# A new step list with paired banks, loads of the first pair on three queues, last tiles through ACT alone

## The chip, the cores and the metric

The kernel runs on one core of one Trainium2 chip. The time is the device time of one execution in microseconds; the median of the runs is compared. The engines are PE (TensorE: matmuls, with its weight loads as PEld), DVE (VectorE), ACT (ScalarE), POOL (GpSimd) and SP (SyncE, which only issues transfers here). DMA queues of SP, ACT and POOL move data between HBM and SBUF; matmul results lie in PSUM.

## The reference

q, k and v are 8 batches x 8 heads x 1152 positions x 64. Neighbouring queries are averaged, so 576 queries meet 1152 keys. The output of attention, 4608 tokens x 512, goes through a multiplicative FFN without a nonlinearity.

```python
q_pool = q.reshape(B, H, S // 2, 2, D).mean(axis=3)
scores = scale * np.matmul(q_pool, k.transpose(0, 1, 3, 2))
attn = softmax(scores)                     # with 1e-9 in the sum
x = np.matmul(attn, v)                     # to [4608, 512]
a = x @ w1; b = x @ w2
out = (a * b @ w3) @ w_out
```

All inputs and outputs are float32; the kernel computes in float16 with float32 sums.

## The kernel before

Two heads make a pair, so there are 32 pairs (four to a batch). The scores of all pairs are one long row of blocks, cut into 324 **slots** of 512 columns for both heads: PE multiplies keys by queries into a two-bank PSUM tile `psc` (L284) and ACT writes the exponential to a ring in SBUF (L289). An **`a` unit** (128 of them, four to a pair) multiplies 128 queries' exponentials by v with a column of ones beside it (L346), and DVE divides (L351, L358); the result is turned into `xT`, by PE for the first eight pairs and by a DMA transpose issued on SP after that (L303). The last 64 queries of two pairs form a **`c` unit** (L373).

The FFN is a list of 196 **steps**: eight "turn" and eight "mult" that form w3 times w_out, then for each of nine chunks of 512 tokens eight times "a" (w1) and "b" (w2), four matmuls of 512 columns each, and four "o" of eight matmuls. An "a" result is copied to `asb`, a "b" result is multiplied by it into `gT`, an "o" result is scaled into `osb` and stored. DVE does these, except in the **tail** (after the last slot), where ACT copies "a", and DVE and ACT each scale half of an "o". The very last step (`fill_last`) runs in two halves of 256 columns.

PSUM has eight banks: three two-bank buffers `psc` (`double()`) and two one-bank buffers `one` (`single()`).

The order on PE is written out by hand in a string, `PLAN`, one letter a step:
- `s`: a slot; `a`: an `a` unit; `c`: a `c` unit; `k`, `j`: turning keys and queries of a pair on PE (`transp_pe`, `transp_rest`); `t`: turning a finished result now.
- `f`: one FFN step in a `one` bank. `F`: one FFN step in a `psc` buffer of which one bank is used. `D`: two FFN steps, one in each half of the same `psc` buffer. `d`: two FFN steps in two `one` banks (not in either plan).

Other engines follow PE's order: their instructions stand in the order in which the string's steps are recorded. The tile framework sets the waits between engines.

For pair 0, loads are split so that a first slot can start early: keys 0 to 2 of nine blocks (`KA = 3`), the two heads' queries `qst0`, and a short rest `qtl0`. ACT casts the first keys (L552), DVE adds neighbouring queries (L555, L556), and PE turns both into one `psc` tile (L246), which is copied out as `kqT` in two pieces (L249).

Of the kernel before, what the change touches and what calls it, by code (L numbers as in the profile page):

```python
# [13 lines left out]

GRP = 2
PLAN = (
    "ksssjsssssksssssfaFasssfsssaksffssasacsssasakassfssfssfassakassfsssffsssffsssafkascsssasaFasssfs"
    "sakassfkssafsssafcsssfFtasssafssaFasssafssafssafssafsssfasscfasssafasssffssfsssafsssafsssafsssaf"
    "fsssafcsssafssafasssaffsssaaFasssffssffssscfasssaffsssafassfsssafsssafsssafassscfasssaaFfsssaffs"
    "ssaffsssaffsssaffssscfasssaaFasssaffsssffsssafsssafsssaasfssscfasssaffsssaffsssaffsssaffsssaffss"  # L20
    "saaFcsssaaFasssaffsssfFasssafsssafasssffssscfasssaffsssaffsssaffsssffFfsssaffsssaaFassscfasssafa"
    "sssafsssfassaassfsssaffsssfaFassscffsssffssffsssafssafasssafassaDaassscfasssafsssfssfasssaffsssa"
    "ffsssaffsssaffsssaaFcsssafFfsssfaDasssaffsssfssaFcFaFaFaFaFFFFFFFFFFFFFFFFFFFFFFFFFFFFFFFFFFFFFF"
)


# [91 lines left out]
def kernel(  # L118
# [11 lines left out]
    nc = tc.nc  # L130
# [14 lines left out]
    QM = 4  # L145
# [98 lines left out]
    def turn_blocks(pt, kq16, blocks):  # L244
        for c in blocks:
            nc.tensor.transpose(pt[:, c * 128:c * 128 + 128], kq16[:, c].rearrange("p u d -> p (u d)"), ident16)  # L246

    def copy_blocks(eng, kqT, pt, c0, c1):
        eng(out=kqT[:, c0:c1].rearrange("p c i -> p (c i)"), in_=pt[:, c0 * 128:c1 * 128])  # L249
# [3 lines left out]
    def transp_pe(p):  # L253
        kq16 = pairs[p]
        kqT = att.tile([128, NB, 128], FP16, tag="kqT", bufs=3)
        pt = double().rearrange("p b c -> p (b c)").bitcast(FP16)
        if p == 0:
            turn_blocks(pt, kq16, list(range(KA)) + list(range(NJ, NB)))
            copy_blocks(nc.vector.tensor_copy, kqT, pt, NJ, NB)
            copy_blocks(nc.scalar.copy, kqT, pt, 0, KA)  # L260
            rest[0] = (kq16, kqT)
        else:
            turn_blocks(pt, kq16, range(NB - 1, -1, -1))
            for c0, c1 in ((8, NB), (0, 4), (4, 8)):
                copy_blocks(nc.vector.tensor_copy, kqT, pt, c0, c1)
        pairs[p] = kq_views(kqT)
# [131 lines left out]
    def pieces(c):  # L398
        a = (c * CH) % XR
        if a + CH <= XR:  # L400
            return [(0, a, CH)]
        return [(0, a, XR - a), (XR - a, 0, CH - (XR - a))]
# [39 lines left out]
                    nc.tensor.matmul(pt[:, d0:d0 + n], wt[:, mc, ft * 128:ft * 128 + 128], xT[:, mc, a:a + n],  # L442
                                     start=(mc == 0 and d0 == 0), stop=(mc == NC - 1), skip_group_check=True)

    def mm_rows(two, pts):
        kind, c, ft = two[0]
        for half in range(2):
            for m in range(NC if kind == "a" else NF):
                for d0, a, n in (pieces(c) if kind == "a" else [(0, 0, dm)]):
                    for u in range(2):  # L450
                        hs = slice(u * 64, u * 64 + 64)
                        x = (half + u) % 2
                        if kind == "a":
                            wt = (w1sb, w2sb)[x]
                            lhsT, rhs = wt[hs, m, ft * 128:ft * 128 + 128], xT[hs, m, a:a + n]
                        else:
                            t0 = two[x][2] * 128
                            lhsT, rhs = gTs[c][hs, m, t0:t0 + 128], T16[hs, m, :]
                        nc.tensor.matmul(pts[x][:, d0:d0 + n], lhsT, rhs, start=(half == 0 and m == 0 and d0 == 0),
                                         stop=(half == 1 and m == (NC if kind == "a" else NF) - 1), skip_group_check=True)  # L460

    def put(step, pt):
        kind, c, ft = step
        tail = st["s"] == NS
        if kind == "turn":
            w3T[ft] = msb.tile([128, NF, 128], FP16, tag="w3T", bufs=2, name="w3T")
            nc.vector.tensor_copy(out=w3T[ft].rearrange("p a i -> p (a i)"), in_=pt.bitcast(FP16))
        elif kind == "mult":
            nc.vector.tensor_copy(out=T16[:, ft, :], in_=pt)
        elif kind == "a":  # L470
            asbs[ft] = msb.tile([128, CH], FP32, tag="asb", bufs=2, name="asb")
            (nc.scalar.copy if tail else nc.vector.tensor_copy)(out=asbs[ft], in_=pt)  # L472
        elif kind == "b":
            nc.vector.tensor_tensor(out=gTs[c][:, ft, :], in0=pt, in1=asbs.pop(ft), op=ALU.mult)  # L474
        else:
            osb = msb.tile([128, dm], FP32, tag="osb", bufs=3, name="osb")
            if tail:
                nc.vector.tensor_scalar_mul(out=osb[:, 0:256], in0=pt[:, 0:256], scalar1=1.0 / (SCL * SCL))
                nc.scalar.mul(out=osb[:, 256:512], in_=pt[:, 256:512], mul=1.0 / (SCL * SCL))
                store(nc.sync, c * CH + ft * 128, osb)  # L480
            else:
                nc.vector.tensor_scalar_mul(out=osb, in0=pt, scalar1=1.0 / (SCL * SCL))  # L482
                store(nc.gpsimd, c * CH + ft * 128, osb)

    def take():
        step = steps[st["f"]]
        st["f"] += 1
        ready(step)
        return step

    def fill_one(bank):
        st["mode"] = 1
        step = take()
        mm(step, bank)
        put(step, bank)

    def fill_last():
        _, c, n = take()
        osb = msb.tile([128, dm], FP32, tag="osb", bufs=3, name="osb")
        for x in range(2):  # L500
            cs = slice(x * 256, x * 256 + 256)
            pt = double()[:, 0, 0:256]
            for f_ in range(NF):
                nc.tensor.matmul(pt, gTs[c][:, f_, n * 128:n * 128 + 128], T16[:, f_, cs],  # L504
                                 start=(f_ == 0), stop=(f_ == NF - 1))
            if x == 0:
                nc.scalar.mul(out=osb[:, cs], in_=pt, mul=1.0 / (SCL * SCL))
            else:
                nc.vector.tensor_scalar_mul(out=osb[:, cs], in0=pt, scalar1=1.0 / (SCL * SCL))
        store(nc.sync, c * CH + n * 128, osb)  # L510

    def fill_two(banks):
        kinds = [s_[0] for s_ in steps[st["f"]:st["f"] + 2]]
        if st["mode"] == 0 and kinds in (["a", "b"], ["o", "o"]):
            two = [take(), take()]
            pts = banks()
            mm_rows(two, pts)
            for step, pt in zip(two, pts):
                put(step, pt)
        else:  # L520
            pts = banks()
            for pt in pts:
                fill_one(pt)


    def w3_load(r):
# [6 lines left out]
    kst0 = att.tile([128, 2, NJ, D], FP32, tag="kst")  # L533
    qst0 = att.tile([128, 2, QM * 2 * D], FP32, tag="qst")
    qtl0 = att.tile([QT, 2, 2 * D], FP32, tag="qtl")
    for u in range(2):
        nc.sync.dma_start(out=qst0[:, u], in_=q[0, u, 0:QM * 256].rearrange("(p c) d -> p (c d)", p=128))
    nc.scalar.dma_start(out=kst0[:, :, 0:KA], in_=k_view(0)[:, :, 0:KA])
    nc.scalar.dma_start(out=qtl0, in_=q[0, 0:2, QM * 256:S].rearrange("u (p t) d -> p u (t d)", t=2))
    nc.sync.dma_start(out=kst0[:, :, KA:NJ], in_=k_view(0)[:, :, KA:NJ])  # L540
    load_kq(1, nc.sync, nc.sync)
# [85 lines left out]
    for op in PLAN:  # L627
        if op == "s":
            slot()
        elif op == "a":  # L630
            av_unit(st["a"])
            st["a"] += 1
            st["mode"] = 1
        elif op == "c":
            av_tails(st["c"])
            st["c"] += 1
            st["mode"] = 2
        elif op == "f":
            fill_one(single())
        elif op == "F":  # L640
            if st["f"] == len(steps) - 1:
                fill_last()
            else:
                fill_one(double()[:, 0, :])
        elif op == "D":
            def banks():
                two = double()
                return two[:, 0, :], two[:, 1, :]
            fill_two(banks)
        elif op == "d":  # L650
            fill_two(lambda: (single(), single()))
        elif op == "k":
            transp_pe(st["k"])
            st["k"] += 1
            st["mode"] = 1
        elif op == "j":
            transp_rest()
            prepare(2)
            st["mode"] = 1
        elif op == "t":  # L660
            one = single()
            turn_mm(one)
            turn_copy(one)
            st["mode"] = 1
        if not flag and st["a"] == NU and st["c"] == (NP // GRP if GRP else 0) and not turns:
            count_bad()
        if "okh" in flag and "badi" not in flag and st["f"] >= len(steps) - 20:
            read_bad()
# [35 lines left out]
```

## Time and profile before

| what | us |
|---|---|
| runs (3): median | 418.66 |
| lowest, highest | 417.94, 419.73 |
| profiled execution | 419.7 |
| its span in the profile | 417.5 |
| PE busy | 399.7 |
| ACT busy | 323.0 |
| DVE busy | 208.8 |

The span runs from the first to the last instruction of the program; 2.2 us of the profiled execution lie around it. Busy times overlap between engines. A line of a timeline gives start, duration, engine, source line, operation, output and inputs, and in brackets how long the engine sat idle before and who released it. A line of the waits gives the waiting instruction, the releaser, the total in us, the count and the longest. L numbers are lines of the kernel before.

### The profile page before, as it was taken

What the parts mean: (1) busy time and instruction counts of PE and PEld (TensorE: products, weight loads), DVE (VectorE), ACT (ScalarE), POOL (GpSimd) and SP (SyncE); (2) the same over time, 40 slices, a digit from 0 to 9 for tenths busy, and PEclk for the clock granted to TensorE, in tenths of its full rate; (3) what the DMA queues carried; (4) which work ended last, traced back from release to release, by engine and by line L of the source; (5) the groups of instructions that cost most, each with busy time, mean ns of one, the idle gap of its engine ahead of it and who ended that gap; (6) DMA issues with size and microseconds to landing.
All of it is one profiled execution on the core that took longest, in us unless ns stands there. A gap on an engine that the chain in (4) does not pass through costs nothing.

```text
span 417.5 us, 12618 instructions
## 1 busy us (share of the span) xinstructions
PE 399.7 (96%) x5273; PEld 231.6 (55%) x5273; DVE 208.8 (50%) x565; ACT 323.0 (77%) x354; POOL 166.8 (40%) x211
## 2 busy tenths in 40 slices
PE   2899999999999999999999999999999999999993
PEld 1466666656556556564556555556776555554442
DVE  1156566666355635654456445644654465453331
ACT  3979897999998998888998889789896886622321
POOL 3979877733173318331635064117430600000000
PEclk9999999999999999999999999999999999999998
DMA  8999998999897999977999689949994910320302
GB/s 258 258 304 275 264 297 298 340 242 308 222 201 207 235 242 304 249 212 200 256 272 280 160 226 290 295 91 292 233 254 98 202 52 15 64 65 0 100 2 108
DMA packets 90895, 86.34 MB, mean 207 GB/s; under 512 B 59664, under 2 KB 64272, under 8 KB 90832
## 3 DMA queue, kind: packets, MB, share of 16 engines
q1 hardware_dynamic: 81616, 59.85, 59.9%
q0 software_dynamic: 8800, 25.37, 21.2%
q8 instruction: 43, 0.70, 0.7%
q10 hardware_dynamic: 416, 0.26, 0.2%
q14 instruction: 20, 0.16, 0.2%
HBM read 67.11 MB, written 9.44 MB: 183 GB/s over the span
## 4 chain that ended last, share of the span: by engine, by line
PE 93%; ACT 3%; DMA 1%; DVE 1%; issue 0%; SPq 0%; DVEq 0%; ACTq 0%
PE one L442 20%; PE psc L284 20%; PE one L346 19%; PE one L436 10%; PE psc L442 10%; PE psc L436 5%; PE one L433 3%; ACT ring L289 3%; PE one L373 3%; PE psc L246 2%; DMA qst<-in_q_dram 1%; PE one L430 1%; PE one L314 0%; PE psc L504 0%; PE psc L433 0%
## 5 line engine op out<-in xcount | busy, mean ns | idle before, releaser
L289 ACT ACTIVATE ring<-psc 128x1024 f16<-128x1024 f32 x324 | 307.1, 1028 | 46.6 <-PE psc L284 46.3
L284 PE MATMUL psc<-kqT 64*128 64x512 f16 (+7 forms) x1152 | 95.6, 291 | 2.8 <-ACT kqT L249 1.1
L346 PEld LDWEIGHTS <-ring 128*128 128x128 f16 x2304 | 79.7, 98 | 26.6 <-issue 17.1
L346 PE MATMUL one<-vaug,ring 128*128 128x65 f16 x2304 | 91.2, 194 | 0.0
L284 PEld LDWEIGHTS <-kqT 64*128 64x128 f16 x1152 | 43.4, 95 | 48.9 <-issue 30.3
L226 POOL CAST kq<-kst 128x1152 f16<-128x1152 f32 x31 | 35.7, 1150 | 58.2 <-DMA kqT<-kq 48.7
L413 POOL DMA_DIRECT2D out_dram<-osb x22 | 12.1, 551 | 110.7 <-DVE osb L482 82.2
L442 PE MATMUL one<-xT,w1sb 128*128 128x512 f16 (+1 forms) x220 | 49.5, 352 | 0.0
L442 PE MATMUL one<-xT,w2sb 128*128 128x512 f16 (+1 forms) x216 | 49.4, 356 | 0.0
L351 DVE RECIPROCAL rzall<-one 128x2 f32<-128x2 f32 x128 | 21.5, 168 | 54.5 <-PE one L346 38.5
L436 PE MATMUL one<-T,gT 128*128 128x512 f16 x192 | 45.4, 379 | 0.0
L442 PEld LDWEIGHTS <-w1sb 128*128 128x128 f16 x320 | 28.3, 97 | 27.2 <-DVE xb L358 3.5
L442 PEld LDWEIGHTS <-w2sb 128*128 128x128 f16 x320 | 28.0, 97 | 25.3 <-issue 2.3
L436 PEld LDWEIGHTS <-gT 128*128 128x128 f16 x280 | 25.5, 98 | 28.9 <-issue 1.5
L472 DVE COPY asb<-one 128x512 f32<-128x512 f32 x48 | 33.2, 691 | 16.5 <-PE one L442 16.5
L474 DVE TENSOR_TENSOR gT<-one,asb 128x512 f16<-128x512 f32 x48 | 33.2, 691 | 16.5 <-PE one L442 16.5
L219 POOL TENSOR_TENSOR kq<-qst 128x512 f16<-128x512 f32 x31 | 39.4, 1271 | 1.6 <-DMA qst<-in_q_dram 1.5
L234 POOL CAST vaug<-vst 128x1152 f16<-128x1152 f32 x32 | 36.6, 1143 | 5.6 <-DMA vst<-in_v_dram 5.5
L482 DVE TENSOR_SCALAR osb<-one 128x512 f32<-128x512 f32 x24 | 16.6, 691 | 34.7 <-PE one L436 34.7
L358 DVE TENSOR_TENSOR xb<-one,rzall 128x128 f16<-128x128 f32 x96 | 28.0, 291 | 3.3
L474 DVE TENSOR_TENSOR gT<-psc,asb 128x512 f16<-128x512 f32 x24 | 16.6, 691 | 18.5 <-PE psc L442 18.5
L442 PE MATMUL psc<-xT,w2sb 128*128 128x512 f16 (+1 forms) x104 | 24.6, 362 | 0.8 <-DVE asb L472 0.8
(71 smaller groups left out, 266.4 us busy)
## 6 DMA issues: line engine op xcount, KB each, us to landing
vst<-in_v_dram SPq DMA_DIRECT2D x25, 576.0 KB, 5.2
kst<-in_k_dram SPq DMA_DIRECT2D x23, 576.0 KB, 6.0
qst<-in_q_dram SPq DMA_DIRECT2D x23, 512.0 KB, 7.6
out_dram<-osb POOLq DMA_DIRECT2D x22, 256.0 KB, 5.7
kst<-in_k_dram POOLq DMA_DIRECT2D x8, 576.0 KB, 9.0
qst<-in_q_dram POOLq DMA_DIRECT2D x8, 512.0 KB, 9.7
vst<-in_v_dram POOLq DMA_DIRECT2D x7, 576.0 KB, 8.0
out_dram<-osb SPq DMA_DIRECT2D x10, 256.0 KB, 2.1
```

What stands on the lines that cost most here:

```text
L219: eng.tensor_tensor(out=kq16[:, NJ:NJ + QM].rearrange("p c u d -> p u c d"), in0=qv[:, :, :, 0], in1=qv[:, :, :, 1], op=ALU.add)
L226: nc.gpsimd.tensor_copy(out=kq16[:, 0:NJ].rearrange("p c u d -> p u c d"), in_=kst)
L234: nc.gpsimd.tensor_copy(out=va[:, :, :, 0:D], in_=vs.pop(p).rearrange("p u (c d) -> p u c d", d=D))
L284: nc.tensor.matmul(psc[:, u, f - s * G:f - s * G + ln], kT2[u * 64:u * 64 + 64, jt, :], qpT[u * 64:u * 64 + 64, i0:i0 + ln], start=True, s ...
L289: nc.scalar.activation(out=ring[:, :, r0:r0 + G], in_=psc, func=AF.Exp, bias=0.0, scale=SCALE)
L346: nc.tensor.matmul(one[:, u * E1:u * E1 + E1], ring[:, u, c0:c0 + 128], va[:, u, jt, :], start=(jt == 0 and u == 0), stop=(jt == NJ - 1), ...
L351: nc.vector.reciprocal(out=rz, in_=av[:, :, D:E1].rearrange("p u o -> p (u o)"))
L358: nc.vector.tensor_tensor(out=xbt, in0=av[:, :, 0:D], in1=rz.unsqueeze(2).to_broadcast([128, 2, D]), op=ALU.mult)
L436: nc.tensor.matmul(pt, gTs[c][:, f_, ft * 128:ft * 128 + 128], T16[:, f_, :], start=(f_ == 0), stop=(f_ == NF - 1))
L442: nc.tensor.matmul(pt[:, d0:d0 + n], wt[:, mc, ft * 128:ft * 128 + 128], xT[:, mc, a:a + n], start=(mc == 0 and d0 == 0), stop=(mc == NC - ...
L472: (nc.scalar.copy if tail else nc.vector.tensor_copy)(out=asbs[ft], in_=pt)
L474: nc.vector.tensor_tensor(out=gTs[c][:, ft, :], in0=pt, in1=asbs.pop(ft), op=ALU.mult)
```

## The change

Four parts.

1. A new `PLAN`. Counts of letters, before and after: `s` 324 and 324, `a` 128 and 128, `c` 16 and 16, `k` 8 and 8, `f` 134 and 128, `F` 58 and 40, `D` 2 and 14, `t` 1 and 2. Behind the last `s` before: `aFcFaFaFaFa` and 38 times `F`. After: `ffcFaDDfaFaffDFFFaFffFDFDFDFFFDfDFFfDDFF`.
2. The special matmul order for two steps at once (`mm_rows`) and the letter `d` are removed; `D` now always runs its two steps one after the other with `fill_one`.
3. Pair 0: the first keys are loaded through POOL's queue, the two heads' queries through SP's and ACT's, one each. PE turns the keys first and ACT copies them, then PE turns the queries and DVE copies them.
4. The end: both halves of the last tile are scaled by ACT, and the stores of the last two tiles are issued by ACT instead of SP.

```diff
@@ PLAN: last two of seven lines
-    "sssafsssfassaassfsssaffsssfaFassscffsssffssffsssafssafasssafassaDaassscfasssafsssfssfasssaffsssa"
-    "ffsssaffsssaffsssaaFcsssafFfsssfaDasssaffsssfssaFcFaFaFaFaFFFFFFFFFFFFFFFFFFFFFFFFFFFFFFFFFFFFFF"
+    "saffsssfasssafsssfasssafssscfasssafFasssaffsssafssaaFfsssaffsssfFfssscfasssafFasssafsssafsssfass"
+    "safsssafcsssaaDfsssaffsssafDfsssaaDasssfDasssffcFaDDfaFaffDFFFaFffFDFDFDFFFDfDFFfDDFF"
...
@@ transp_pe, p == 0
-            turn_blocks(pt, kq16, list(range(KA)) + list(range(NJ, NB)))
-            copy_blocks(nc.vector.tensor_copy, kqT, pt, NJ, NB)
-            copy_blocks(nc.scalar.copy, kqT, pt, 0, KA)
+            turn_blocks(pt, kq16, range(KA))
+            copy_blocks(nc.scalar.copy, kqT, pt, 0, KA)
+            turn_blocks(pt, kq16, range(NJ, NB))
+            copy_blocks(nc.vector.tensor_copy, kqT, pt, NJ, NB)
...
@@ put, "o" in the tail
-                store(nc.sync, c * CH + ft * 128, osb)
+                store(nc.scalar if st["f"] >= len(steps) - 1 else nc.sync, c * CH + ft * 128, osb)
...
@@ fill_last
-            if x == 0:
-                nc.scalar.mul(out=osb[:, cs], in_=pt, mul=1.0 / (SCL * SCL))
-            else:
-                nc.vector.tensor_scalar_mul(out=osb[:, cs], in0=pt, scalar1=1.0 / (SCL * SCL))
-        store(nc.sync, c * CH + n * 128, osb)
+            nc.scalar.mul(out=osb[:, cs], in_=pt, mul=1.0 / (SCL * SCL))
+        store(nc.scalar, c * CH + n * 128, osb)
@@ fill_two
-        kinds = [s_[0] for s_ in steps[st["f"]:st["f"] + 2]]
-        if st["mode"] == 0 and kinds in (["a", "b"], ["o", "o"]):
-            two = [take(), take()]
-            pts = banks()
-            mm_rows(two, pts)
-            for step, pt in zip(two, pts):
-                put(step, pt)
-        else:
-            pts = banks()
-            for pt in pts:
-                fill_one(pt)
+        for pt in banks:
+            fill_one(pt)
@@ first loads
-    for u in range(2):
-        nc.sync.dma_start(out=qst0[:, u], in_=q[0, u, 0:QM * 256].rearrange("(p c) d -> p (c d)", p=128))
-    nc.scalar.dma_start(out=kst0[:, :, 0:KA], in_=k_view(0)[:, :, 0:KA])
+    nc.gpsimd.dma_start(out=kst0[:, :, 0:KA], in_=k_view(0)[:, :, 0:KA])
+    for u, eng in enumerate((nc.sync, nc.scalar)):
+        eng.dma_start(out=qst0[:, u], in_=q[0, u, 0:QM * 256].rearrange("(p c) d -> p (c d)", p=128))
     nc.scalar.dma_start(out=qtl0, in_=q[0, 0:2, QM * 256:S].rearrange("u (p t) d -> p u (t d)", t=2))
     nc.sync.dma_start(out=kst0[:, :, KA:NJ], in_=k_view(0)[:, :, KA:NJ])
@@ D
-            def banks():
-                two = double()
-                return two[:, 0, :], two[:, 1, :]
-            fill_two(banks)
-        elif op == "d":
-            fill_two(lambda: (single(), single()))
+            two = double()
+            fill_two((two[:, 0, :], two[:, 1, :]))
```

More of the change, by code (lines that the diff above doesn't have):

```diff
@@ L16 @@
 PLAN = (
[L17 to L21, printed above, removed]
-    "sssafsssfassaassfsssaffsssfaFassscffsssffssffsssafssafasssafassaDaassscfasssafsssfssfasssaffsssa"
-    "ffsssaffsssaffsssaaFcsssafFfsssfaDasssaffsssfssaFcFaFaFaFaFFFFFFFFFFFFFFFFFFFFFFFFFFFFFFFFFFFFFF"
+    "ksssjsssssksssssfaFasssfstssaksafsssfasscsassaksafsssffsssfassaksafsssfssaFacsssfasssfakkassfsss"
+    "afsssftFkssafsssfFasssafcsssafssfassafssfasssafssaFasssfFasssfassaFcsssafsssfasssfasssafsssafssf"
+    "FasssafcsssffssfassafssfasssafassfasssafcsssfFasssafassfasssafsssafsssfasssafsssafcsssafssafasss"
+    "faFasssffssffsssaffsssaaFcsssfFfsssaaFasssfssfsssfasssfasssaffssscfasssaffsssafassaassffsssaffss"
+    "safcsssaaFasssaffsssaffsssafsssfasssfasssafsssffcsssfFfsssfFasssaaFasssaffsssaaFcsssfFasssaaFass"
+    "saffsssfasssafsssfasssafssscfasssafFasssaffsssafssaaFfsssaffsssfFfssscfasssafFasssafsssafsssfass"
+    "safsssafcsssaaDfsssaffsssafDfsssaaDasssfDasssffcFaDDfaFaffDFFFaFffFDFDFDFFFDfDFFfDDFF"
 )
@@ L443, in mm @@
                                      start=(mc == 0 and d0 == 0), stop=(mc == NC - 1), skip_group_check=True)
[L445 to L449, printed above, removed]
-                    for u in range(2):
[L451 to L455, printed above, removed]
-                        else:
[L457 to L460, printed above, removed]
     def put(step, pt):
@@ L505, in fill_last @@
                                  start=(f_ == 0), stop=(f_ == NF - 1))
-            if x == 0:
-                nc.scalar.mul(out=osb[:, cs], in_=pt, mul=1.0 / (SCL * SCL))
-            else:
-                nc.vector.tensor_scalar_mul(out=osb[:, cs], in0=pt, scalar1=1.0 / (SCL * SCL))
-        store(nc.sync, c * CH + n * 128, osb)
-    def fill_two(banks):
-        kinds = [s_[0] for s_ in steps[st["f"]:st["f"] + 2]]
-        if st["mode"] == 0 and kinds in (["a", "b"], ["o", "o"]):
-            two = [take(), take()]
-            pts = banks()
-            mm_rows(two, pts)
-            for step, pt in zip(two, pts):
-                put(step, pt)
-        else:
-            pts = banks()
-            for pt in pts:
-                fill_one(pt)
+            nc.scalar.mul(out=osb[:, cs], in_=pt, mul=1.0 / (SCL * SCL))
+        store(nc.scalar, c * CH + n * 128, osb)
+    def fill_two(banks):
+        for pt in banks:
+            fill_one(pt)
     def w3_load(r):
@@ L535 @@
     qtl0 = att.tile([QT, 2, 2 * D], FP32, tag="qtl")
-    for u in range(2):
-        nc.sync.dma_start(out=qst0[:, u], in_=q[0, u, 0:QM * 256].rearrange("(p c) d -> p (c d)", p=128))
-    nc.scalar.dma_start(out=kst0[:, :, 0:KA], in_=k_view(0)[:, :, 0:KA])
+    nc.gpsimd.dma_start(out=kst0[:, :, 0:KA], in_=k_view(0)[:, :, 0:KA])
+    for u, eng in enumerate((nc.sync, nc.scalar)):
+        eng.dma_start(out=qst0[:, u], in_=q[0, u, 0:QM * 256].rearrange("(p c) d -> p (c d)", p=128))
     nc.scalar.dma_start(out=qtl0, in_=q[0, 0:2, QM * 256:S].rearrange("u (p t) d -> p u (t d)", t=2))
```

## Prediction

> **What bounds the kernel now.** I read the page first: shares, slices, chain.
>
> ```profile
> span 417.5 us, 12618 instructions
> PE 399.7 (96%) x5273; PEld 231.6 (55%) x5273; DVE 208.8 (50%) x565; ACT 323.0 (77%) x354; POOL 166.8 (40%) x211
> PE   2899999999999999999999999999999999999993
> ACT  3979897999998998888998889789896886622321
> PE 93%; ACT 3%; DMA 1%; DVE 1%; issue 0%; SPq 0%; DVEq 0%; ACTq 0%
> ```
>
> PE is busy in every slice but the first two and the last, and the chain that ended last is PE for 93%. So what counts is how long PE takes through its own list, where it waits, how early it starts and what follows its last matmul. A busy PE need not be at its peak, so next I put the PE's matmuls beside the plan, letter by letter, and measured each step from its first matmul to the next step's. After 24 us the same pair of neighbours takes the same time nearly everywhere: a four-matmul step 0.86, an eight-matmul step 1.73, an `a` 0.56; a slot's two to four matmuls 0.23. Entering a run of slots costs 0.09 and leaving it 0.09. Both plans hold the same 5273 matmuls.
>
> Then the waits of PE from 24 to 365 us, and from 365 us on. The first answer has two rows, the second none:
>
> ```profile
> PE psc L442 <- DVE gT L474: 0.8, 1, 0.8
> PE psc L442 <- DVE asb L472: 0.8, 1, 0.8
> ```
>
> These are the only two places where PE stands still after the start, and they are exactly the two `D` in the plan of before. The timeline around the second:
>
> ```profile
> 350.45 1.02 PE L442 MATMUL psc<-xT,w1sb 128*128 128x512 f16 x4
> ...
> 351.51 0.69 DVE L472 COPY asb<-psc 128x512 f32<-128x512 f32 x1 [0.32 <-PE psc L442]
> 352.25 1.02 PE L442 MATMUL psc<-xT,w2sb 128*128 128x512 f16 x4 [0.78 <-DVE asb L472]
> ```
>
> A `D` takes one two-bank `psc` buffer and runs two FFN steps into its halves. The second step does not follow at 350.45 + 0.86 = 351.31. It starts when the copy out of the first half is over, at 352.25: **0.94 us lost**. The other `D` took 1.82 (311.57 to 313.39) against 0.88 for its neighbours: 0.94 again. Single steps (`f`, `F`) take a fresh buffer each; the 38 `F` that close the plan of before, from 370.56 us on, ran without a gap.
>
> **The `D` steps.** The new plan has 14 in place of 2; 10 of them stand after the last slot, where nothing but FFN steps is left. In the built list of the changed kernel, the first matmul of every one of the 14 second halves carries a wait on DVE or ACT, the engine that reads the first half. Nothing can cover it: PE goes through its list in order, and behind the waiting matmul stands all the rest of PE's work. What the first half is decides the price:
> - 4 before the last slot, copy or product by DVE as in the row: 4 x 0.94 = 3.76.
> - 4 in the tail begin with an "a" step, which ACT copies in 0.58 instead of 0.69: 0.94 - 0.11 = 0.83, x4 = 3.32.
> - 3 begin with a "b". DVE's product took 0.69, but began 0.12 after the matmuls' end (373.15 + 1.03 to 374.29) instead of 0.04: about 1.01, x3 = 3.03.
> - 3 begin with an "o", read by DVE and then by ACT, one after the other:
>
> ```profile
> 384.58 0.42 DVE L478 TENSOR_SCALAR osb<-psc 128x256 f32<-128x256 f32 x1 [0.97 <-PE psc L436]
> 385.03 0.38 ACT L479 ACTIVATE osb<-psc 128x256 f32<-128x256 f32 x1 [2.46 <-DVE osb L478]
> 371.62 0.58 ACT L472 COPY asb<-psc 128x512 f32<-128x512 f32 x1 [2.24 <-PE psc L442]
> ```
>
> From 384.58 to 385.41 is 0.83 in place of 0.69: 1.08, x3 = 3.24. (The last row is the 0.58 used above.)
>
> Sum 13.35; less the two of before (1.88): **+11.5 us**. No row of before shows two `D` in succession, which the new plan has twice; both ends there are "no more than the sum" and, were a third buffer late, one more 0.9.
>
> **The rest of the list.** Runs of slots fall from 119 to 118: -0.2. A tail unit `c` followed by one single-bank step and an `a` makes the `a` wait 0.1 for the `c`'s bank (0.96 instead of 0.86); this pattern falls from 8 to 3: -0.5. An extra early `t` moves two small matmuls. The removed two-bank row-split matmuls were not reached by the plan of before. Hidden waits of the new order are bounded from below by 0, since before had none to remove, and from above by rows for what could come late: the transposed kq lands 6.7 us after its issue (median), and in the new list at least 8.5 us of PE work lie between issue and use (9.2 before); the first FFN step of a chunk stands 13 us or more behind the last `a` that feeds it through a DMA transpose (10.9 before; median landing 4.5, worst 9.5). I take 0, and keep 3 us for the range. ACT has 20% of its time free and hides the reordered exponentials.
>
> **The start.** The rows up to the first slot:
>
> ```profile
> 5.28 0.51 ACT L552 CAST kq<-kst 128x384 f16<-128x384 f32 x1 [1.98 <-DMA kst<-in_k_dram]
> 6.60 0.71 PE L246 MATMUL psc<-ident,kq 128*128 128x128 f16 x5 [0.25 <-DVE kq L555]
> 7.35 0.49 DVE L249 COPY kqT<-psc 128x640 f16<-128x640 f16 x1 [0.58 <-PE psc L246]
> 7.87 0.48 ACT L249 COPY kqT<-psc 128x384 f16<-128x384 f16 x1 [2.08 <-DVE kqT L249]
> 8.41 1.46 PE L284 MATMUL psc<-kqT 64*128 64x512 f16 x10 [1.09 <-ACT kqT L249]
> ```
>
> Before, the late second half of q sets the first slot: added at 6.54, turned, copied twice in a row. With keys first, ACT's copy comes ahead of the query turns, and as built these turns wait for it (one `psc` tile again). The new chain is: keys land, cast 0.51, three turns 0.50, ACT copy 0.48, five turns 0.71, DVE copy 0.49, and five hand-overs of about 0.05: 2.94 from the landing of the keys to the first slot. The keys' first part now goes through POOL's queue. No row shows that transfer there; the nearest ones:
>
> ```profile
> kst<-in_k_dram ACTq DMA_DIRECT2D x1, 192.0 KB, 4.5
> w3c<-in_moe_w_dram POOLq DMA_DIRECT2D x4, 512.0 KB, 7.5
> ```
>
> Lower bound: 4.5 as on ACT's queue, landing at 5.25, first slot at 8.2, 0.2 earlier than before. Upper bound: the fastest 512 KB load on POOL's queue, 6.4, landing at 7.15, first slot at 10.1, +1.7. I take the middle, 5.5: **+0.8**. All of it reaches the end, since from there ACT's and PE's work follow one upon the other. The transfer's issue (0.7 to 0.9 on POOL) pushes the identity and memsets to about 3 us, ahead of their use at 5.85; were that cover gone it would cost those 0.8. Q halves on two queues land together rather than one after the other; they are no longer last.
>
> **The end.** Last matmul, then copy, issue, landing. The last half goes to ACT (0.38) instead of DVE (0.42 at 410.75), and ACT issues its store itself, saving a hand-over of 0.06: -0.1. The store before it is now issued by ACT too, 0.3 to 0.5 between ACT's pieces of the last two tiles; the first of these ended 0.5 before the last matmul, so this room is just enough: 0, at worst +0.1. I take 0 for the two together.
>
> **Sum.** +11.5 - 0.2 - 0.5 + 0.8 = +11.6. The profiled execution took 419.7 (span 417.5 and 2.2 around it), so it would become 431.3. The median of before, 418.66, lies 1.0 under that execution: predicted **430.2 us**.
>
> **Rivals.**
> 1. *The two halves of a `D` do not block each other.* They lie in different banks; if the wait were met when PE comes to it, both the 12 new and the two old stalls vanish: 418.66 - 1.9 - 0.7 + 0.8 = 416.9, with the start's lower bound 415.9. This is the other side, and it decides where the reader's end comes before PE's 0.22 per matmul runs out. Against it: the two rows of waits and the built waits. Chance 0.05, 0.02 of it faster by over 0.5%. The Trainium skill, "PSUM — Partial Sum Buffer", section "PSUM bank collisions raise a hardware error", asks for ordering by bank and quadrant only and calls different banks clean; by that no wait is needed, and the time would be this rival's. The trace has the program order whole tiles all the same: 0.78 us of waiting for a reader of the other bank.
> 2. *The PE clock falls in the tail.* PE turned 128-wide blocks every 0.107 us up to 22.9 us, with gaps of 0.3 to 1 us in its work, and every 0.056 after; it reached that pace only after 3.2 us without a gap. If ten gaps of about 1 us put it back for some 3 us each, at half pace, 1.5 us apiece: +15, 445. Against: the pace stayed at 0.216 per 512 columns after both gaps of before. Chance 0.04. The Trainium skill, "TensorE: Matmul & The Clock Gate", section "A second HAM failure mode: psum-queue depth-cycling", tells of such falls from frequent short idling between groups of matmuls. The single gaps of before neither show nor exclude it.
> 3. *The new order has waits of its own* (a late transpose, an exponential not ready): 3 to 6 us more, 433 to 436. Chance 0.06.
> 4. *Half the stalls are absorbed*, say since DVE and ACT are idle enough in the tail to read sooner: +6, 424. But the durations used are already those of idle engines. Chance 0.04.
>
> **How the numbers follow.** The forecast, 427 to 433, holds 0.81. Range 426.5 to 433.5: the unknown of the start (-1.0, +0.9), hidden waits (+3) and the spread of the runs (about 1), less a fifth of the shares on each `D`. Half a percent, 2.1 us, is about what can be told from no change. Slower: forecast, 2, 3 and 4, 0.95; faster 0.02; same 0.03.
>
> **What would show it.** PE's waits after 24 us should list 14 rows' worth of second halves, about 0.8 to 1.1 each, ten behind the last slot; the first slot between 8.2 and 10.1; steps elsewhere at 0.86 and 1.73. It is wrong if the second halves of `D` start 0.86 or 1.73 after the first, if matmuls in the tail come slower than 0.216, or if PE waits elsewhere.

## The result, and the profile after

The changed kernel took 430.06 us (median of 4 runs, 427.5 to 430.61), the kernel before 418.58 (4 runs) beside it: ratio 1.0259, 95% interval 1.0212 to 1.0306. It is 11.5 us slower. The profiled execution took 429.98 with a span of 427.8, so span against span it is 10.3 more.

From the page of the changed kernel, the span, PE's busy slices and the shares of the chain that ended last:

```profile
span 427.8 us, 12633 instructions
PE   1899999999999999999999999999999988898885
PE 92%; ACT 3%; DVE 2%; DMA 1%; issue 1%; DVEq 0%; POOLq 0%
```

Where PE before had a 9 in every slice between the start and the last, now seven of the last eight show an 8 or a 5: most of the loss lies in the last fifth. The chain shows DVE at 2% instead of 1%: PE stands behind it. PE's waits from 24 us on say for whom (waiting instruction, releaser, total us, times, longest):

```profile
PE psc L443 <- DVE gT L458: 4.0, 5, 0.9
PE psc L437 <- ACT osb L463: 2.8, 3, 0.9
PE psc L443 <- ACT asb L456: 2.7, 4, 0.7
PE psc L437 <- DVE gT L458: 0.9, 1, 0.9
PE psc L443 <- DVE asb L456: 0.8, 1, 0.8
```

5 + 3 + 4 + 1 + 1 are 14 waits, one for each `D`, and there is no other row. (The rows count idle time from the modelled end of the last matmul; the loss against an undisturbed step is 0.16 more each.) Two of them in the timeline of the tail, first an "a" and its "b", then two "o":

```profile
403.37 1.03 PE L443 MATMUL psc<-xT,w1sb 128*128 128x512 f16 x4
...
404.43 0.59 ACT L456 COPY asb<-psc 128x512 f32<-128x512 f32 x1 [1.09 <-PE psc L443]
405.07 0.38 PE L443 MATMUL psc<-xT,w2sb 128*128 128x512 f16 x1 [0.67 <-ACT asb L456]
...
414.68 1.89 PE L437 MATMUL psc<-T,gT 128*128 128x512 f16 x8
...
416.61 0.42 DVE L462 TENSOR_SCALAR osb<-psc 128x256 f32<-128x256 f32 x1 [0.96 <-PE psc L437]
417.07 0.38 ACT L463 ACTIVATE osb<-psc 128x256 f32<-128x256 f32 x1 [3.30 <-DVE osb L462]
...
417.50 0.38 PE L437 MATMUL psc<-T,gT 128*128 128x512 f16 x1 [0.93 <-ACT osb L463]
```

The "b" starts 1.70 after the "a" instead of 0.86: 0.84 lost. The second "o" started 2.82 after the first instead of 1.73: 1.09. Taken matmul by matmul, the 14 losses add up to 13.45 us; the two of before were 1.88.

The start of the changed kernel, first the transfer of the first keys (size, us to landing) and then its timeline:

```profile
kst<-in_k_dram POOLq DMA_DIRECT2D x1, 192.0 KB, 6.4
```

```profile
1.30 0.87 POOL L508 DMA_DIRECT2D kst<-in_k_dram  x1 [0.84 <-POOLq L656]
```

```profile
7.69 0.51 ACT L524 CAST kq<-kst 128x384 f16<-128x384 f32 x1 [4.48 <-DMA kst<-in_k_dram]
8.26 0.50 PE L246 MATMUL psc<-ident,kq 128*128 128x128 f16 x3 [8.26 <-ACT kq L524]
8.79 0.48 ACT L249 COPY kqT<-psc 128x384 f16<-128x384 f16 x1 [0.59 <-PE psc L246]
9.32 0.69 PE L246 MATMUL psc<-ident,kq 128*128 128x128 f16 x5 [0.57 <-ACT kqT L249]
10.13 0.49 DVE L249 COPY kqT<-psc 128x640 f16<-128x640 f16 x1 [3.06 <-PE psc L246]
10.67 1.46 PE L285 MATMUL psc<-kqT 64*128 64x512 f16 x10 [0.66 <-DVE kqT L249]
```

The keys land at 7.7, and each of the five pieces waits for the one above it: the first slot starts at 10.67, 2.27 later than in the profile of before. POOL's queue moved its first packet at 5.87, so 4.6 of the 6.4 passed before any of the keys' data moved.

The end: the transfers that SP issues last, in the changed kernel and in the kernel before (start, us to the end of the last issue), and ACT's last in the changed kernel:

```profile
417.48 3.21 SPq L414 DMA_DIRECT2D out_dram<-osb  x2
...
423.31 0.34 ACTq L414 DMA_DIRECT2D out_dram<-osb  x1
```

```profile
408.09 3.49 SPq L413 DMA_DIRECT2D out_dram<-osb  x3
```

The program closes with a value that the engines read from SBUF and branch on (`values_load` and `tc.If` in the kernel). SP's own waits, before and after, have these rows, in which it waits for itself at that branch:

```profile
SPq L672 <- SPq L672: 2.7, 1, 2.7
```

```profile
SPq L640 <- SPq L640: 4.1, 3, 2.6
```

Before, SP ended its last issue at 411.58, then read that value, branched, stood 2.7 us and closed the program at 417.5, 5.9 after that issue. The last store had landed at 413.73, 1.5 before SP went on at 415.26: the pause, not the store, decided. After, SP was through with its stores at 420.69, so the branch and its pause (the 2.6 of the 4.1; the other two waits come behind it) ran beside the last tile; ACT's store ended its issue at 423.65 and the program 4.2 later. Here SP went on at 424.23 and waited for the last landing, 426.05. From the first matmul of the last step to the end it is 6.9 us instead of 8.8.

### The profile page after: what moved, and what is told of

It reads as the page before. It is cut to its first block, busy times and chain, and to the rows that moved or that the text cites. A ratio compares the mean times of both kernels' runs of the same rounds, so it can differ in the third digit from the quotient of the medians.

```text
span 427.8 us, 12633 instructions
## 1 busy us (share of the span) xinstructions
PE 400.2 (94%) x5273; PEld 233.6 (55%) x5273; DVE 206.6 (48%) x564; ACT 324.1 (76%) x356; POOL 167.1 (39%) x211
## 4 chain that ended last, share of the span: by engine, by line
PE 92%; ACT 3%; DVE 2%; DMA 1%; issue 1%; DVEq 0%; POOLq 0%
PE psc L285 19%; PE one L443 19%; PE one L347 18%; PE psc L443 11%; PE one L437 10%; PE psc L437 4%; PE one L434 3%; PE one L374 3%; PE psc L246 2%; DMA kst<-in_k_dram 1%; ACT ring L290 1%; DVE gT L458 1%; PE one L431 1%; ACT asb L456 1%; PE one L315 0%
## 5 line engine op out<-in xcount | busy, mean ns | idle before, releaser
L347 PEld LDWEIGHTS <-ring 128*128 128x128 f16 x2304 | 81.3, 98 | 26.8 <-issue 14.2
L437 PE MATMUL one<-T,gT 128*128 128x512 f16 x200 | 47.4, 380 | 0.0
L443 PE MATMUL one<-xT,w2sb 128*128 128x512 f16 (+2 forms) x188 | 42.3, 352 | 0.0
L414 POOL DMA_DIRECT2D out_dram<-osb x21 | 11.6, 554 | 76.6 <-DVE osb L466 59.8
L456 DVE COPY asb<-one 128x512 f32<-128x512 f32 x44 | 30.4, 692 | 22.3 <-PE one L443 22.3
L458 DVE TENSOR_TENSOR gT<-one,asb 128x512 f16<-128x512 f32 x41 | 28.4, 692 | 19.7 <-PE one L443 19.7
L443 PE MATMUL psc<-xT,w2sb 128*128 128x512 f16 (+2 forms) x132 | 31.8, 366 | 3.5 <-ACT asb L456 2.7
L458 DVE TENSOR_TENSOR gT<-psc,asb 128x512 f16<-128x512 f32 x31 | 21.4, 692 | 23.0 <-PE psc L443 22.9
```

The costliest lines, as they stand in the source:

```text
L347: nc.tensor.matmul(one[:, u * E1:u * E1 + E1], ring[:, u, c0:c0 + 128], va[:, u, jt, :], start=(jt == 0 and u == 0), stop=(jt == NJ - 1), ...
L437: nc.tensor.matmul(pt, gTs[c][:, f_, ft * 128:ft * 128 + 128], T16[:, f_, :], start=(f_ == 0), stop=(f_ == NF - 1))
```

## The experiments

Theory: each `D` costs the time that the reader of its first half needs, because its two halves are one buffer to the program; the start costs 2 to 3 us by the keys' queue; the end gives back 1.8. Rivals: the new order is slow in itself; the late start is made up later; the end saves only a hand-over. All ran on one chip per group with the kernel before beside them (418.7 to 419.0 us).

**Two buffers for each `D`.** Changed kernel, every `D` of `PLAN` as two `F`:

```diff
-D
+FF
```

> The changed kernel with every D of its plan replaced by two F: the same FFN steps in the same order, each in a buffer of its own. Theory (a second half waits for the reader of the first): the 14 stalls, 13.4 us in the trace of the changed kernel, go, and no others come; 430.1 - 13.4 = 416.7 us, PE's waits after 24 us under 1 us in total. Rival (the new order itself is slow, the waits only lie where others would): 420 or more. Rival (three two-bank buffers are too few for so many F): single stalls of up to 0.9 us each in the tail, 418 to 422.

415.91 us (414.5 to 416.61, 6 runs), ratio to before 0.9922 (95% interval 0.9896 to 0.9947). PE's waits from 24 us on have no row at all. The last step's first matmul came at 407.46 instead of 420.95. So the 14 stalls were the pairing of banks, not the new order, and three two-bank buffers are enough.

**Ten `D` in the old list.** Kernel before, its tail with ten `FF` rewritten as `D`, each an "a" with its "b"; with its own two it holds 12. The end of the string:

```diff
-FFFFFFFFFFFFFFFFFFFFFFFFFFFFFFFFFFFFFF
+DDDDDDDFFFFDDDFFFFFFFFFFFFFF
```

> The kernel before with ten pairs of F in its tail written as D, each an 'a' with its 'b' (four or more after each other); the order of the steps is the same. Theory (every second half waits for the reader of the first, whatever list it stands in): ten stalls of 0.84 with ACT's copy in between, 419.0 + 8.4 = 427.4 us, first slot and end as before. Rival (the stalls belong to the new order, or successive D hide one another): 419 to 422 us.

427.79 us (426.86 to 428.49, 4 runs), ratio 1.0209 (1.019 to 1.0228), 9.0 us more than before. Its waits of PE from 24 us on:

```profile
PE psc L442 <- ACT asb L472: 6.7, 10, 0.7
PE psc L246 <- POOL kq L221: 1.1, 1, 1.1
PE one L430 <- DMA w3c<-in_moe_w_dram: 0.8, 1, 0.8
PE psc L442 <- DVE gT L474: 0.8, 1, 0.8
PE psc L442 <- DVE asb L472: 0.8, 1, 0.8
```

Ten waits more in the tail, each second half 0.84 late, 8.4 in all, also where seven `D` stood in succession. The second and third rows, at 26.9 and 29.0 us, are waits for inputs that the profile of before does not have; they are not of `D`. The stall goes with the letter in either list.

**The start of before.** Changed kernel with the loads and the turning of before (the two start pieces of the change's diff undone).

> The changed kernel with the loads and turns of pair 0 as before. Theory (the keys through POOL's queue set the first slot): first slot back from 10.7 to 8.4 us, 430.1 - 2.3 = 427.8 us. Rival (the late first slot is made up later, as ACT paces the first 20 us): 430 us, the first slot at 8.4 all the same. The 14 stalls of the D steps stay at 13.4 us under both.

426.75 us (426.27 to 427.59, 5 runs), 3.3 under the changed kernel, by the ratios to before on each chip (1.0197 against 1.0259) 2.6; the two ratios' intervals, 1.0173 to 1.0221 and 1.0212 to 1.0306, just touch. First slot at 7.58, and all 14 stalls still there, 13.45. The late start is not made up. The profiled kernel of before had its first slot at 8.41, the slowest of its runs; other profiles with the same loads and turning have it at 7.37 to 8.11, those with POOL's load and one buffer at 10.34 to 10.67, so the start costs 2.2 to 3.3 between them.

**Which part of the start.** Changed kernel, only the loads undone:

```diff
-    nc.gpsimd.dma_start(out=kst0[:, :, 0:KA], in_=k_view(0)[:, :, 0:KA])
-    for u, eng in enumerate((nc.sync, nc.scalar)):
-        eng.dma_start(out=qst0[:, u], ...)
+    for u in range(2):
+        nc.sync.dma_start(out=qst0[:, u], ...)
+    nc.scalar.dma_start(out=kst0[:, :, 0:KA], in_=k_view(0)[:, :, 0:KA])
```

> The changed kernel with the three loads of pair 0 on the queues of before (keys on ACT's, both halves of q on SP's); the keys are still turned and copied first. Theory (the queue of the keys is what costs): the keys land near 5.2 instead of 7.7 us, first slot 2.9 to 3.0 after them or 1.7 to 1.9 after the queries' last addition, 7.7 to 8.4; 427 to 428 us. Rival (the serial turns and copies are what costs): first slot above 9.5, 429 us or more.

426.0 us (425.39 to 427.46, 4 runs; ratio 1.0168, 1.0142 to 1.0195), first slot at 7.33, keys cast at 4.35: a little better than expected, as the keys landed earlier than in the profile of before. The queues of the loads carry the whole loss, and by the chain above it is that of the keys. Turning keys first does no harm where the keys come before the queries (1.40 us from the end of the last addition of queries, L528, to the first slot, against 1.65 in the profile of before).

Changed kernel with its own loads, keys and queries in two `psc` buffers:

```diff
+            pq = double().rearrange("p b c -> p (b c)").bitcast(FP16)
             turn_blocks(pt, kq16, range(KA))
+            turn_blocks(pq, kq16, range(NJ, NB))
             copy_blocks(nc.scalar.copy, kqT, pt, 0, KA)
-            turn_blocks(pt, kq16, range(NJ, NB))
-            copy_blocks(nc.vector.tensor_copy, kqT, pt, NJ, NB)
+            copy_blocks(nc.vector.tensor_copy, kqT, pq, NJ, NB)
```

> The changed kernel with its own loads (keys through POOL's queue), keys and queries turned into two psc buffers. The queries are then turned and copied before the late keys come. Theory (waiting goes by whole buffers): the first slot comes 1.6 us after the keys land (cast 0.51, three turns 0.50, copy 0.48, hand-overs) instead of 3.0, so about 9.3; 430.1 - 1.4 = 428.7 us. Rival (the keys' landing alone decides): first slot as in the changed kernel, 10.5 us.

429.01 us (428.64 to 429.34, 4 runs); first slot 9.65, 2.18 after the keys' cast began, against 2.98. From the cast to the first slot 0.80 is saved where 1.4 was expected, and the runs overlap those of the changed kernel: the waits on the shared buffer went, but PE still turns the queries behind the keys in its list, so that DVE's copy comes last.

**The end.** The changed kernel with the end of before, and the kernel before with the new end (the last two pieces of the change's diff).

> The changed kernel with the last tiles scaled and stored as before (last half by DVE, stores by SP). Theory (SP's reading of the check value, its branch and the 2.6 us that follow come only after its last store, so they stand at the end of the program): from the last step's first matmul to the end 8.7 us instead of 6.9, 430.1 + 1.8 = 431.9 us. The prediction's own reckoning (only a hand-over of 0.06 saved): 430.1 us, no change.

> The kernel before with only the new end (last tile scaled by ACT, the last two stores issued by ACT). Theory as for the old end in the changed kernel, now the other way: 418.6 - 1.8 = 416.8 us, from the last step's first matmul to the end 6.9 us instead of 8.7. The prediction's own reckoning: 418.5 us.

431.63 us (429.88 to 431.94, 6 runs) and 416.67 us (415.07 to 418.78, 12 runs; ratio 0.9948, 0.993 to 0.9965). From the last step's first matmul to the end: 8.6 with SP's stores and 6.7 with ACT's. So the new end is worth 1.6 to 2.4 us, both ways round, where the prediction had 0.

Then the kernel before with ACT issuing the stores and the last half still scaled by DVE. The kernel that ran moves the stores of both last tiles, not only the last as its expectation says.

> The kernel before with one change: the last tile's store is issued by ACT instead of SP; it is still scaled by ACT and DVE. Theory (SP's branch and its 2.6 us stand behind its last store): SP gets past its check value earlier only as far as its then last store, that of the tile before (issued near 409.8 instead of 411.2), so 1.4 of the 1.8 us: 418.9 - 1.4 = 417.5 us. Rival (the scaling by ACT alone saves it): 418.9 us.

417.39 us (416.45 to 418.44, 11 runs; ratio 0.9965, 0.995 to 0.998): 1.65 saved; from the last step's first matmul to the end 7.5, against 6.7 with the whole new end and 8.8 before. The stores are the larger part. What ACT's scaling adds, 0.8 in the traces, is more than the 0.16 by which its store is issued earlier. SP's waits of this run say where the rest comes from:

```profile
SPq L699 <- DVEq L672: 0.8, 1, 0.8
```

As DVE still scales the last half, it comes to its own branch only at 410.1 and stands 3.65 us behind it, to 413.85; the last store had landed at 412.4. With ACT scaling both halves (the kernel before with the whole new end) DVE branches at 409.0, goes on at 412.01, and the landing, 412.99, comes last. So the new end takes two pauses off the close of the program, SP's and DVE's.

**The best of both.** The changed kernel with `FF` for `D` and the start of before; the kernel before with `FF` for its `D` and the new end; and the first of these with two buffers at the start.

> The changed kernel with each D as two F and the start of before; the new end stays. If the parts add: 415.9 (two F) - 2.3 to 3.3 (start) = 412.6 to 413.6 us. If the start's gain and the D's stalls overlap: 415 or more.

> The kernel before, its own list with its two D as two F each, and the new end. If the parts add: 416.7 - 1.9 = 414.8 us. Against the version with the new list it tells what the new order is worth by itself: by the rows about 1 to 1.6 us (fewer waits of an a for a c's bank, two waits of slots less); if nothing, both come to the same time.

> The changed kernel with each D as two F, the loads of before, and pair 0's keys and queries turned into two psc buffers in place of one, so that neither copy nor turn waits for the other. Theory (the buffer is the unit of waiting): from the last addition of the queries to the first slot 1.3 us instead of 1.65 to 1.9, so 0.4 us less than the version with the start of before, 412.2 to 413.2 us. Rival (another landing sets the first slot): no difference.

413.53 us (412.65 to 414.26, 4 runs; ratio 0.9873, 0.9853 to 0.9893), 415.31 (414.21 to 415.6, 6 runs; 0.9913, 0.9898 to 0.9928) and 412.51 (411.75 to 414.28, 5 runs; 0.9857, 0.9835 to 0.9878). The parts add within half a us. New list against old with nothing else different: 1.8 us, and 2.04 between first slot and last step in the traces. Of these, 0.76 is one wait of the old list for a load of w3 (at 28.6 us) that the profile of before does not have. The start with two buffers:

```profile
5.73 0.48 ACT L250 COPY kqT<-psc 128x384 f16<-128x384 f16 x1 [0.59 <-PE psc L247]
...
5.97 0.71 PE L247 MATMUL psc<-ident,kq 128*128 128x128 f16 x5 [0.27 <-DVE kq L529]
6.72 0.49 DVE L250 COPY kqT<-psc 128x640 f16<-128x640 f16 x1 [0.62 <-PE psc L247]
7.26 1.46 PE L287 MATMUL psc<-kqT 64*128 64x512 f16 x10 [0.58 <-DVE kqT L250]
```

ACT's copy now starts before the queries are turned instead of standing behind DVE's, and the first slot starts at 7.26 instead of 7.78 with the same landings (first addition at 4.10 and 4.09). The medians agree in sign, but their runs overlap. This version has the lowest median here, 6.2 us under the kernel before.

## Why the prediction was right or wrong

- **The `D` steps: right.** +11.5 forecast, 13.45 - 1.88 = +11.57 measured; the prices by kind, 0.94, 0.83, 1.01 and 1.08, came as 0.94, 0.84, 1.01 and 1.09. Two runs show the cause: without `D` no wait is left, and `D` in the old list brings them there.
- **The start: mechanism right, size wrong.** The chain from the keys' landing was put at 2.94 and took 2.98. What failed is the term "I take the middle, 5.5" and the bounds around it: the transfer was counted from 0.75, but POOL issued it at 1.30, and it took 6.4, the upper bound's own figure. Those 0.55 + 0.9 are the difference between the forecast +0.8 and the +2.27 of the two profiles; the first slot, 10.67, fell outside "between 8.2 and 10.1".
- **The end: wrong.** The forecast followed the last tile only: copy, issue, landing, 0 in sum. Measured 8.8 to 6.9 us. What it left out is SP's pause behind its branch, which stood in SP's waits of before as 2.7 us and in the program's close behind its last store, and DVE's, which comes to the fore once SP's is out of the way.
- **The rest of the list:** -0.7 forecast. In the traces it is 12.20 (last step) - 11.57 - 2.27 = -1.64; the pattern of `c`, one step and `a` is down from eight to three, as forecast, and three early waits of slots (0.70 together at 26, 39 and 123 us, each too short for a row of the waits) are gone, which the forecast had not counted. By the two lists run alike, the new order by itself is 1.8 us better.
- **The sum.** The start was missed by +1.5, the end by -1.9 and the rest by -0.9; the first two nearly cancel, and span against span +10.3 came where +11.6 was forecast. The median was met (430.2 against 430.06) also because 1.0 had been taken off for the profiled execution of before, which lay above its median, while that of after lay on it. The size and cause of the `D` term were right; that the time came within 0.2 us is luck.
- **Rivals.** Banks that do not block each other: refuted by the 14 waits; with buffers of their own the same steps run without one. The Trainium skill, "PSUM — Partial Sum Buffer", section "PSUM bank collisions raise a hardware error", calls different banks clean; the version with `FF` agrees, 415.91 us and no wait. The falling clock: between the stalls the tail's matmuls kept 0.216 us per 512 columns (0.86 a step), with ten gaps of 0.8 to 1.1 us in 50 us, and the trace records no fall of the granted clock before the program's end. The Trainium skill, "TensorE: Matmul & The Clock Gate", section "A second HAM failure mode: psum-queue depth-cycling", tells of a fall by such idling; it did not show here. Waits of the new order's own: none in PE's waits from 24 us on. Half the stalls absorbed: no, each cost its full price.

## What to carry to other kernels

A buffer of several banks is one thing to a program that orders by buffer: before two results share it, compare the reader's time with the time of the second producer, and take two buffers if there are enough. One step that stands still can be priced from a single row of the profile and multiplied, if nothing else runs on that engine. Read the waits of the engines that close the program too: what each does after its last transfer or copy is part of the time.

## What was not expected of the hardware

The first transfer on POOL's queue at the program's start took 6.0 to 6.4 us for 192 KB in the four profiles that have it, where ACT's took 3.4 to 4.5 for the same 192 KB in the other nine, and was issued 0.55 later. Its first packet moved 4.2 to 4.6 us after the issue began, on ACT's queue 1.8 to 2.2 us after; why is not shown. SP's branch at the end was followed by 2.5 to 2.7 us without an instruction in each of these profiles and DVE's by 2.9 to 3.7, where ACT's took 0.4. What the engines do in that time no run here tests; it cost nothing only where a later landing of another engine's store hid it.
